# Two decode layers on one core: unread matmuls in three places, and the operand roles of the last up projection

## The chip, the cores and the metric

The kernel runs on one core of one Trainium2 chip. The metric is the device time of one execution in microseconds (us). The core has a matrix engine (PE, TensorE), a vector engine (DVE), a scalar engine (ACT), a general engine (POOL, GpSimd), and a queue (SP) from which nearly all of this kernel's transfers are issued. Matmul results go to PSUM, which the code uses as eight banks of 128 partitions by 512 fp32 numbers; the other engines read them there. A profile of the PE shows two rows, the matmuls (PE) and the loads of the stationary operand (PEld). The granted clock of the PE is shown too: 1.00 is full speed.

## The reference

The model has the sequence attention, feed-forward, attention, feed-forward, with a residual sum around each and one set of weights and caches for both layers. Batch is B = 4, one query token each, D = 512, 32 query heads on 8 key/value heads of 128, 4096 cached positions, feed-forward width F = 1792. All inputs are bf16.

```python
def _A_ref(x, k_cache, v_cache, wq, wo):
    q = heads(x @ wq); k = repeat(k_cache, 4); v = repeat(v_cache, 4)
    p = softmax(einsum("bhqd,bhkd->bhqk", q, k) * Dh ** -0.5)
    return merge(einsum("bhqk,bhkd->bhqd", p, v)) @ wo

def _B_ref(x, w_gate, w_up, w_down):
    return (gelu(x @ w_gate) * (x @ w_up)) @ w_down

x = A_x
x = x + _A_ref(layernorm(x), ...)
x = x + _B_ref(layernorm(x), ...)
x = x + _A_ref(layernorm(x), ...)
x = x + _B_ref(layernorm(x), ...)
```

(`heads`, `repeat` and `merge` stand for the reshapes that are cut here.)

## The kernel before, in words

The key and value caches are 67 MB in all and are read from memory as tiles of 512 KB: 16 positions by 128 numbers on each of 128 partitions. The batch entries go through the layers one after another. The first attention of entry 0 is `attend_first`, its feed-forward is `dense_first`; `attend(b, ...)` works on the second attention of entry b - 1 and the first attention of entry b together, with the keys of an entry kept on the chip between its two attentions; `dense(b, ...)` is the feed-forward of entry b in layer 1. The last entry's second attention is `attend_last`, and the second feed-forward is done once for all four entries in `dense_last`. The order of instructions on every engine is the order of the Python text: the schedule is written by hand (`manual_schedule`), and each engine takes its instructions in that order, waiting on semaphores that the tile framework adds between producers and consumers. The framework keeps tiles apart, so a tile that fills a PSUM bank counts as one thing.

A matmul has a stationary operand (`lhsT`, loaded first) and a moving operand (`rhs`). The kernel uses both ways round for products of activations and weights:

- **weights as the stationary operand** (`mac`, `ffn_in`, `OutProj.heads`, `q_heads`): a 128x128 block of weights is loaded, and a few activation columns, repeated up to 32 or 64 (`wide`), move through it. One matmul for each block; the result has its features on the partitions. For one 512 by 1792 projection that is 14 x 4 = 56 matmuls (`ffn_in`, KF = 14 column blocks by KD = 4 row blocks).
- **weights as the moving operand** (`streamed`, `rows_of` in `dense_last`): a few activation columns are loaded, and 448 columns of weights move. Four such matmuls fill four groups of 32 partitions, j = 0 to 3. For a projection that is 4 x 4 = 16 matmuls. The result has the batch on the partitions and the features along the free axis, and a DVE transpose within 32x32 blocks (line 1365 and 1370) turns it. Because the transpose reads all 128 partitions and only four in each group of 32 are written, the bank is first filled with zeros by ACT (`nothing`, line 346).

`busy(count, unread, ...)` (line 460) issues matmuls of 128 rows by up to 512 columns into a part of PSUM that nobody reads. They have the identity as the stationary operand and the gate weights as the moving one.

**Where the change touches it.**

`dense_first` (line 1260 on) ends with `down`, 56 matmuls of weight blocks into the bank `whole` (tile name y), then one unread matmul of 384 columns into the rest of that same bank. What follows in the main loop is `add_x` (line 396, DVE: XX + y, rounded into xb), then `stats` (line 182: four matmuls of xb against itself for mean and mean square, into a small tile st of the pool ps_sm), then `add_y` (line 401). After that `Early.queries` makes the queries of the second attention, whose first scores set free the key slots for which the SP queue waits (line 489).

`attend_last` (line 1203 on) works through the value tiles with `vals.step`. For all heads but the last, the value tile is the moving operand (line 752, tile so); a DVE transpose (line 760), a reduction (line 767) and a multiplication (line 768) follow and give the head outputs OT2_bf (OT_bf in the profile's names). The last head takes the value tile as the stationary operand (line 819, tile ot) and is scaled in line 651. Output projections: the first three groups of heads go through `RowProj` (line 377, tile yr, weights moving), which `split` takes out of PSUM (ACT line 383, DVE line 384); the last group goes through `OutProj` (line 253, tile y, weights stationary), and `onto` adds the rows to it. Between these stand three calls of `busy` on a bank `spare` of the pool ps_h: four matmuls behind the first two row projections, one behind the third, and one behind the last `proj.heads`.

The last value tiles come from transfers issued late: two heads' tiles as one transfer of 1024 KB each into slots of the query weights (`pump_head`, line 685), and the last head's two tiles into key slots, one whole (line 673) and one in two halves (line 679).

`dense_last` (line 1311 on): the bank u is filled with zeros by ACT, then add_x, stats and add_y for all four entries; DVE prepares the shifts (line 1335) and the variance, POOL takes it to the power -0.5 (line 188). PE runs the 16 gate matmuls (line 1320, tile gr) and the 16 up matmuls (line 1320, tile u), then clears two tiles and turns x back (lines 1355 and 1359, tile xr). DVE: transpose of gr (1365), minus shift (1366), times rstd (1367); ACT: gelu (1369); DVE: transpose of u (1370), minus shift (1371), product with the gelu (1373). PE: the 56 down matmuls (line 1359, tile yo). DVE: the sum with x (1382), and then four small transfers out.

Of the kernel before, what the change touches and what calls it, by code (L numbers as in the profile page):

```python
# [8 lines left out]
FP32 = mybir.dt.float32  # L9
# [6 lines left out]
P = 128  # L16
# [3 lines left out]
QS = P // QD  # L20
WIDE = 32
# [14 lines left out]
def kernel(  # L36
# [13 lines left out]
    nc = tc.nc  # L50
    B, Sq, D = A_x.shape
# [6 lines left out]
    KD = D // P  # L58
    KF = F // P
# [114 lines left out]
        n = shape[0] * shape[1]  # L174
        return (w_sb[:, at].bitcast(FP32)[:, :n].rearrange("p (a b) -> p a b", b=shape[1]))

    def stats(b0, nb):
        st = ps_sm.tile([P, nb, 2], FP32, name="st", tag="sm")
        for i in range(nb):
            b = b0 + i  # L180
            for k in range(KD):
                nc.tensor.matmul(st[:, i], lhsT=xb[:, k, b:b + 1].broadcast_to([P, P]),
                                 rhs=xb[:, k, b:B + 1:B - b],
                                 start=k == 0, stop=k == KD - 1, skip_group_check=True)
        return st
# [159 lines left out]
    def nothing(t):  # L345
        nc.scalar.copy(out=t, in_=qb[:, 0:1].broadcast_to([P, t.shape[1]]))
# [110 lines left out]
    def busy(count, unread, by=None, start=True):  # L457
        rhs = wg_sb[:, 0] if by is None else by
        for _ in range(count):
            nc.tensor.matmul(unread, lhsT=ident_bf[:], rhs=rhs[:, :unread.shape[1]], start=start,  # L460
                             stop=start, skip_group_check=True)

    def down(nb, H_bf, whole):
        y = acc([KD, WIDE], "y2", whole)
        for c in range(KF):
            if c == WD_PARTS[1]:
                busy(2, whole[:, KD * WIDE:], start=False)
            for k in range(KD):
                mac(y[:, k], wd_sb[:, c, k * P:(k + 1) * P], wide(H_bf[:, c, :]),
                    c == 0 and k == 0, c == KF - 1)  # L470
        return y[:, :, :nb]
# [731 lines left out]
    def attend_last(q_bf, norm, before, late):  # L1203
        b = B - 1
        gx, gy = second_groups[b]
        prob2 = {}
        kept2, own2, other2, apart2 = two(b)
        tiles = kept2 + own2 + apart2 + other2
        vals = Values(2, b, tiles, prob2, dst2(b),
                      streamed=[h for h in range(Hkv) if h != tiles[-1][0]],  # L1210
                      paired=[h for h in range(Hkv) if h // 2 != tiles[-1][0] // 2])
        sc2 = [new_scores(early=True)]
        scores(sc2[0], gx, 0)
        ring.pump_tile(late[0], k_tile(gx * GH + 2, 0))
        ring.pump_halves(late[1], k_tile(gx * GH + 3, 0))
        scores(sc2[0], gx, 1)
        q_spread_apart(q_sums(q_bf[:]))
        p0 = soft(sc2[0], norm)
        for _ in range(2):
            before.fill()  # L1220
        before.turn()
        sc2.append(new_scores(early=True))
        scores(sc2[1], gy, 0)
        scores(sc2[1], gy, 1)
        soft_turn(p0)
        before.sum()
        pe0, den0 = soft_swap(p0), soft_den(p0)
        p1 = soft(sc2[1], norm, lasting=True)
        prob2[gx] = (pe0, soft_recip(den0))
        rows = RowProj(o2)  # L1230
        vals.step(8, hold=True)
        soft_turn(p1)
        vals.flush()
        pe1, den1 = soft_swap(p1), soft_den(p1)
        prob2[gy] = (pe1, soft_recip(den1))
        heads = pairs(tiles)
        full = ps_x.tile([P, KF, WIDE], FP32, name="gr", tag="x")
        nothing(full.rearrange("p c r -> p (c r)"))
        nc.scalar.preload_act_table_set("gelu_apprx_tanh_and_others")
        vals.step(4)  # L1240
        rows.heads(heads[0], hp)
        rows.heads(heads[1], hp)
        spare = ps_h.tile([P, 512], FP32, name="spare", tag="h")
        busy(4, spare[:])
        vals.step(2)
        rows.heads(heads[2], hp)
        busy(1, spare[:])
        rows.split()
        vals.step()
        proj = OutProj(o2, B)  # L1250
        proj.heads(heads[3], rep)
        vals.step()
        rows.onto(proj)
        proj.n = Hq - rep
        proj.heads(heads[3] + rep, rep)
        busy(1, spare[:])
        assert vals.left() == 0 and ring.at == len(ring.seq)
        return proj.y, full

    def dense_first(y, scr):  # L1260
        b0, nb, n = 0, 1, 2 * RUN

        def rhs(k):
            return xb[:, k, :n]

        def out_of(i, v):
            nc.vector.tensor_scalar(out=cs_f[:, i], in0=v[:, :, B], scalar1=float(D), scalar2=None,
                                    op0=ALU.mult)
            return v[:, :, b0:b0 + nb]

        add_x(b0, nb, y)
        st = stats(b0, nb)
        add_y(b0, nb, y)
        rstd, mr = ln_scale(nb, st)
        whole = bank("g")
        g = out_of(0, ffn_in(rhs, wg_sb, "g", whole))
        sq = gelu(scr, g, shifts(scr, mr, 0), rstd)
        whole = bank("u")
        busy(6, whole[:])
        u = ffn_in(rhs, wu_sb, "u", whole)  # L1280
        whole = bank("y2")
        busy(4, whole[:])
        u = out_of(1, u)
        H_bf = gate_up(scr, sq, u, shifts(scr, mr, 1), rstd)
        y = down(nb, H_bf, whole)
        busy(1, whole[:, KD * WIDE:], start=False)
        return y

    def dense(b0, y, prev, scr):
        nb = 1  # L1290
# [18 lines left out]
        return turn_rows(y)  # L1309

    def dense_last(y, full):
        up = acc([KF, WIDE], "u")
        nothing(up.rearrange("p c r -> p (c r)"))

        def rows_of(w_sb, full):
            flat = full.rearrange("p c r -> p (c r)")
            for k in range(KD):
# [8 lines left out]
        st = stats(0, B)  # L1326
# [20 lines left out]
        shift(1)  # L1347

        g_rows = rows_of(wg_sb, full)
        u_rows = rows_of(wu_sb, up)  # L1350
        xr = ps_sm.tile([P, P], FP32, name="xr", tag="sm")
        yo = ps_sc.tile([P, P], FP32, name="yo", tag="sc")
        zero = qb[:, 0:1].broadcast_to([P, P])
# [13 lines left out]
        nc.vector.tensor_tensor(out=t[0], in0=t[0], in1=rows(rstd, KF, B), op=ALU.mult)  # L1367
        sq = apart(wq_sb[0], shape, 2)
        nc.scalar.activation(out=sq, in_=t[0], func=ACT.Gelu_apprx_tanh)
        nc.vector.transpose(out=u_rows, in_=u_rows)  # L1370
        nc.vector.tensor_tensor(out=t[1], in0=up[:, :, :B], in1=t[1], op=ALU.subtract)
        H_bf = wq_sb[1][:, 1, :KF * B].rearrange("p (c b) -> p c b", b=B)
        nc.vector.tensor_tensor(out=H_bf, in0=t[1], in1=sq, op=ALU.mult)
# [22 lines left out]
    for b in range(B):  # L1396
        y = dense(b, y, prev, Scratch()) if b else dense_first(y, scr)
        gx, gy = second_groups[b]
        add_x(b, 1, y)
        raw = q_rows(b, gx) if b else None  # L1400
        st = stats(b, 1)
        add_y(b, 1, y)

        if b == 0:
            ring.pump()
            norm = early.queries(b, st)
        else:
            q_bf = q_tile()
            if b == B - 1:
                late = [(2, b) + u for u in two(b)[2]]  # L1410
                room = [[wq_sb[g][:, k].rearrange("p (c d) -> p c d", d=Dh) for k in range(KD)]
                        for g in (gx, gy)]
                pairs_of = [wq_sb[g][:, k:k + NT].rearrange("p t (c d) -> p t c d", d=Dh)
                            for g, k in ((gx, NT), (gy, 0), (gy, NT))]
                ring.pump_head(late[:NT], pairs_of[0])
                prev.fill()
                rest, steps = acc([HG, WIDE], "q"), q_steps(b, gy)
                streamed_part(rest, steps, range(KD // 2))
                banks.back_brief(room[0][0])
            raw = turn_rows(raw)  # L1420
            norm = Norm(st)
            q_round(q_bf, raw, gx, norm)
            if b < B - 1:
                prev.fill()
            norm.root()
            qe = q_sums(q_bf[:])
            if b < B - 1:
                prev.fill()
            else:
                streamed_part(rest, steps, range(KD // 2, KD))  # L1430
                ring.pump_head(late[NT:2 * NT], pairs_of[1])
                ring.pump_head(late[2 * NT:3 * NT], pairs_of[2])
            q_spread(qe)
            if b < B - 1:
                ring.extend(1, b + 1, one(b + 1)[:ahead_of[b + 1]])
                ring.pump()
            else:
                q_bf = q_tile()
                q_round(q_bf, turn_rows(rest), gy, norm)
        if b:  # L1440
            norm.scales()
        if b == B - 1:
            banks.back(room[0][1])

        def qy(b=b, g=gy, norm=norm):
            q_bf = q_tile()
            q_round(q_bf, turn_rows(q_rows(b, g)), g, norm)
            return q_bf[:]

        if b < B - 1:  # L1450
            y, prev = attend(b + 1, qy, prev, norm, early if b == 0 else None)
        else:
            y, full = attend_last(q_bf, norm, prev, late[3 * NT:])
# [32 lines left out]
```

## Time and profile before

| what | value |
|---|---|
| median of 3 runs | 270.87 us (269.98 to 271.11) |
| the profiled execution | 270.28 us, of which the span from first to last instruction is 268.5 us |
| mean granted PE clock over the span | 0.917 |
| PE matmul rows | 199.0 us busy, 4078 matmuls |
| DVE | 176.8 us busy, 435 instructions |
| ACT | 63.2 us busy, 124 instructions |
| memory traffic | 103.10 MB, 384 GB/s on average |
| unread matmuls in `attend_last` (tile spare) | 6, 379 ns median of one row |
| last projections in `dense_last` (line 1320) | gr 16 matmuls, 0.93 us; u 16 matmuls, 0.93 us |
| transpose of u (line 1370) | 0.66 us |

How to read it: a row's duration runs from the start of the first instruction of a group to the modelled end of the last, so neighbouring rows on the PE overlap; the step from one row's start to the next row's start is what a group takes of the PE. The chain of waits is followed back from the last instruction: each of its pieces released the next. DMA issue instructions have a start on the SP queue and a time to landing, counted from that start.

### The profile page before, as it was taken

What the parts mean: (1) busy time and instruction counts of PE and PEld (TensorE: products, weight loads), DVE (VectorE), ACT (ScalarE), POOL (GpSimd) and SP (SyncE); (2) the same over time, 40 slices, a digit from 0 to 9 for tenths busy, and PEclk for the clock granted to TensorE, in tenths of its full rate; (3) what the DMA queues carried; (4) which work ended last, traced back from release to release, by engine and by line L of the source; (5) the groups of instructions that cost most, each with busy time, mean ns of one, the idle gap of its engine ahead of it and who ended that gap; (6) DMA issues with size and microseconds to landing.
All of it is one profiled execution on the core that took longest, in us unless ns stands there. A gap on an engine that the chain in (4) does not pass through costs nothing.

```text
span 268.5 us, 9180 instructions
## 1 busy us (share of the span) xinstructions
PE 199.0 (74%) x4078; PEld 123.6 (46%) x4078; DVE 176.8 (66%) x435; ACT 63.2 (24%) x124; POOL 3.9 (1%) x10
## 2 busy tenths in 40 slices
PE   1395256679689796889688867697799696888893
PEld 1333134568366544447336244364372344544661
DVE  3493952150226899885769997737779987368853
ACT  1001000200404412033315320314235203055620
POOL 2000000000001000000000000000000000000001
PEclk9999557559799979999999988999999989999999
DMA  7999999999996999999999999999999999999920
GB/s 253 420 417 421 417 420 419 411 382 403 407 401 236 391 416 420 417 417 416 377 411 418 417 420 417 417 419 403 403 421 416 417 418 419 416 372 396 416 78 3
DMA packets 32575, 103.10 MB, mean 384 GB/s; under 512 B 2836, under 2 KB 8728, under 8 KB 32536
## 3 DMA queue, kind: packets, MB, share of 16 engines
q1 hardware_dynamic: 32512, 102.51, 95.5%
q8 instruction: 32, 0.52, 0.7%
q14 instruction: 7, 0.06, 0.1%
q10 hardware_dynamic: 24, 0.01, 0.0%
HBM read 102.50 MB, written 0.00 MB: 382 GB/s over the span
## 4 chain that ended last, share of the span: by engine, by line
DMA 48%; DVE 19%; PE 18%; SPq 9%; ACT 2%; issue 2%; DVEq 0%
DMA v_t<-in_A_v_cache_dram 28%; DMA kp<-in_A_k_cache_dram 16%; DVE kp L508 9%; PE sc L563 4%; SPq L149 4%; PE ot L819 4%; DMA wd_sb<-in_B_w_down_dram 4%; SPq L154 3%; PE y L253 3%; PE so L752 2%; PE q L281 1%; DVE q L287 1%; SPq L150 1%; DVE qb L332 1%; DVE pe L573 1%
## 5 line engine op out<-in xcount | busy, mean ns | idle before, releaser
L508 DVE STREAM_TRANSPOSE kp<-kp 128x1024 f32<-128x1024 f32 x64 | 74.1, 1208 | 0.0
L563 PE MATMUL sc<-kp,qb 128*32 128x512 bf16 x512 | 63.4, 429 | 7.3 <-DVE kp L508 3.0
L819 PE MATMUL ot<-pe,v_t 128*128 128x32 bf16 (+1 forms) x1120 | 36.7, 183 | 15.4 <-DMA v_t<-in_A_v_cache_dram 13.1
L819 PEld LDWEIGHTS <-v_t 128*128 128x128 bf16 x1120 | 34.0, 99 | 24.5 <-DMA v_t<-in_A_v_cache_dram 16.1
L563 PEld LDWEIGHTS <-qb 128*32 128x32 bf16 x512 | 21.4, 100 | 39.4 <-issue 21.1
L585 ACT ACTIVATE pe<-sc,nl 128x512 bf16<-128x512 f32 x8 | 5.5, 687 | 85.5 <-DVE pe L582 76.7
L618 PE MATMUL x<-pe,ident_bf 128*32 128x128 bf16 x192 | 5.4, 233 | 12.9 <-DVE pe L593 12.8
L760 DVE STREAM_TRANSPOSE so<-so 128x256 f32<-128x256 f32 (+1 forms) x19 | 11.1, 586 | 5.7 <-PE so L752 5.5
L253 PEld LDWEIGHTS <-wo_sb 128*128 128x128 bf16 x256 | 12.9, 99 | 3.1 <-DMA wo_sb<-in_A_wo_dram 2.5
L253 PE MATMUL y<-OT_bf,wo_sb 128*128 128x64 bf16 x192 | 11.7, 215 | 2.1 <-DMA wo_sb<-in_A_wo_dram 1.8
L618 PEld LDWEIGHTS <-ident_bf 128*32 128x32 bf16 x256 | 5.3, 100 | 16.9 <-issue 14.9
L573 DVE TENSOR_REDUCE pe<-sc 128x1 f32<-128x512 f32 x12 | 8.3, 690 | 6.5 <-PE sc L563 6.4
L752 PE MATMUL so<-v_t,pl 128*32 128x256 bf16 x192 | 9.4, 275 | 3.2 <-DMA v_t<-in_A_v_cache_dram 3.0
L621 ACT CAST pe<-x 128x512 bf16<-128x512 f32 x12 | 7.0, 585 | 19.2 <-PE x L618 19.2
L651 DVE TENSOR_TENSOR OT_bf<-ot,rden 128x8 bf16<-128x8 f32 (+1 forms) x20 | 3.0, 156 | 12.7 <-PE ot L819 12.6
L460 PEld LDWEIGHTS <-ident_bf 128*128 128x128 bf16 x136 | 7.8, 99 | 7.2 <-issue 4.4
L253 PE MATMUL q<-xb,wq_sb 128*128 128x5 bf16 (+1 forms) x192 | 5.5, 170 | 7.5 <-DMA wq_sb<-in_A_wq_dram 7.5
L396 DVE TENSOR_TENSOR xb<-XX,y 128x4 bf16<-128x4 f32 (+1 forms) x9 | 1.6, 173 | 13.6 <-PE y L253 10.8
L752 PE MATMUL so<-v_t,pe 128*32 128x256 bf16 x192 | 7.9, 274 | 2.7 <-ACT pe L621 1.4
L593 DVE STREAM_TRANSPOSE pe<-pe 128x512 bf16<-128x512 bf16 x12 | 8.4, 697 | 2.0 <-ACT pe L585 2.0
L325 PE MATMUL qe<-q_bf,ident_bf 128*32 128x16 bf16 (+1 forms) x272 | 5.5, 175 | 5.6 <-DVE q_bf L307 2.9
L253 PEld LDWEIGHTS <-wq_sb 128*128 128x128 bf16 x192 | 5.2, 98 | 8.1 <-DMA wq_sb<-in_A_wq_dram 8.0
(155 smaller groups left out, 252.0 us busy)
## 6 DMA issues: line engine op xcount, KB each, us to landing
v_t<-in_A_v_cache_dram SPq DMA_DIRECT2D x97, 512.0 KB, 8.5
kp<-in_A_k_cache_dram SPq DMA_DIRECT2D x56, 512.0 KB, 10.1
wq_sb<-in_A_wq_dram SPq DMA_DIRECT2D x2, 2048.0 KB
wo_sb<-in_A_wo_dram SPq DMA_DIRECT2D x4, 1024.0 KB, 11.4
kp<-in_A_k_cache_dram SPq DMA_DIRECT2D x4, 1024.0 KB, 8.6
wq_sb<-in_A_v_cache_dram SPq DMA_DIRECT2D x3, 1024.0 KB, 11.6
wg_sb<-in_B_w_gate_dram SPq DMA_DIRECT2D x1, 1792.0 KB, 12.4
wu_sb<-in_B_w_up_dram SPq DMA_DIRECT2D x1, 1792.0 KB
```

The lines of the kernel that those rows point to most:

```text
L149: dq.dma_start(out=wo_sb[:, i * n:(i + 1) * n], in_=wo_dram[:, i * n:(i + 1) * n])
L154: dq.dma_start(out=wd_sb[:, lo:hi], in_=wd_dram[:, lo:hi])
L253: nc.tensor.matmul(dst, lhsT=lhsT, rhs=rhs, start=first, stop=last, skip_group_check=True)
L460: nc.tensor.matmul(unread, lhsT=ident_bf[:], rhs=rhs[:, :unread.shape[1]], start=start, stop=start, skip_group_check=True)
L508: nc.vector.transpose(out=words, in_=words)
L563: nc.tensor.matmul(sc[s * QS:(s + 1) * QS], lhsT=qb[:, w0:w0 + 2 * W], rhs=kt[:, :, be // 2, :, be % 2], start=(t == 0 and be == 0), stop= ...
L573: nc.vector.tensor_reduce(out=m, in_=sc.rearrange("p c j -> p (c j)"), axis=AX.X, op=ALU.min if norm else ALU.max)
L593: nc.vector.transpose(out=flat, in_=flat)
L618: nc.tensor.matmul(x[a * QS:(a + 1) * QS, s], lhsT=ident_bf[:, s * QS:(s + 1) * QS], rhs=pT[:, a], start=True, stop=True, skip_group_check ...
L752: nc.tensor.matmul(ps[d, :NW * QS], lhsT=x[:, w:w + NW].rearrange("p c h -> p (c h)"), rhs=v[:, i:i + NW, d], start=first and i == 0, stop ...
L760: nc.vector.transpose(out=flat, in_=flat)
L819: nc.tensor.matmul(self.ot[:, s % 2], lhsT=v[:, i, :], rhs=wide(pe[:, s, t * CH + i, :], self.ot.shape[-1]), start=(done == 0 and i == 0), ...
```

## The change

Three edits.

1. `stats` gets an option `spare`, used for entry 0 in the main loop: st is then cut from a whole bank of ps_sm, and one unread matmul of 448 columns goes into the rest of that bank ahead of the four matmuls of the statistics. In `dense_first` the unread matmul of 384 columns behind the down projection goes.
2. In `attend_last` the four unread matmuls behind the second row projection and the one behind the third go. The one behind the last projection stays.
3. In `dense_last` the up projection is done by `ffn_in` with the weights as the stationary operand: 56 matmuls in place of 16. The zeros for its bank (ACT) and the DVE transpose of u go, and the bank is taken after the gate matmuls.

```diff
-    def stats(b0, nb):
-        st = ps_sm.tile([P, nb, 2], FP32, name="st", tag="sm")
+    def stats(b0, nb, spare=False):
+        if spare:
+            whole = ps_sm.tile([P, 512], FP32, name="st", tag="sm")
+            busy(1, whole[:, 2 * QS:])
+            st = whole[:, :2 * nb].rearrange("p (b i) -> p b i", i=2)
+        else:
+            st = ps_sm.tile([P, nb, 2], FP32, name="st", tag="sm")
...
         rows.heads(heads[0], hp)
         rows.heads(heads[1], hp)
-        spare = ps_h.tile([P, 512], FP32, name="spare", tag="h")
-        busy(4, spare[:])
         vals.step(2)
         rows.heads(heads[2], hp)
-        busy(1, spare[:])
         rows.split()
         vals.step()
         proj = OutProj(o2, B)
@@
         proj.heads(heads[3] + rep, rep)
+        spare = ps_h.tile([P, 512], FP32, name="spare", tag="h")
         busy(1, spare[:])
...
         H_bf = gate_up(scr, sq, u, shifts(scr, mr, 1), rstd)
-        y = down(nb, H_bf, whole)
-        busy(1, whole[:, KD * WIDE:], start=False)
-        return y
+        return down(nb, H_bf, whole)
...
     def dense_last(y, full):
-        up = acc([KF, WIDE], "u")
-        nothing(up.rearrange("p c r -> p (c r)"))
...
         g_rows = rows_of(wg_sb, full)
-        u_rows = rows_of(wu_sb, up)
+        up = ffn_in(lambda k: xb[:, k, :B], wu_sb, "u", None)
...
         nc.scalar.activation(out=sq, in_=t[0], func=ACT.Gelu_apprx_tanh)
-        nc.vector.transpose(out=u_rows, in_=u_rows)
         nc.vector.tensor_tensor(out=t[1], in0=up[:, :, :B], in1=t[1], op=ALU.subtract)
...
-        st = stats(b, 1)
+        st = stats(b, 1, spare=b == 0)
```

## The prediction

> **What bounds the kernel now.** I read the page first, then the chain of waits, then the rows in order of time around the three places, then the transfers that land last, and at the end the granted clock. By the page no engine is the bound over the whole span, and the chain is made of all of them:
>
> ```profile
> PE 199.0 (74%) x4078; PEld 123.6 (46%) x4078; DVE 176.8 (66%) x435; ACT 63.2 (24%) x124; POOL 3.9 (1%) x10
> DMA 48%; DVE 19%; PE 18%; SPq 9%; ACT 2%; issue 2%; DVEq 0%
> ```
>
> So each edit is judged in its own stage. The chain of waits (start, us, what) at the three places:
>
> ```profile
> 79.22 0.19 PE y L460
> 79.43 0.18 DVE xb L396
> ...
> 254.62 0.86 PE yr L377 x16
> 255.49 0.97 PE spare L460 x4
> 256.46 0.55 PE so L752 x16
> 257.01 0.43 PE yr L377 x8
> 257.44 0.32 PE spare L460
> 257.76 0.48 PE ot L819 x16
> ...
> 263.11 0.58 DVE u L1370
> 263.71 0.23 DVE wq_sb L1371
> 264.02 0.23 DVE wq_sb L1373
> 264.29 0.98 PE yo L1359 x56
> ```
>
> The reader is to see that the work taken away (the unread matmul at 79.22, the five at 255.49 and 257.44, the transpose at 263.11) is itself a link of the chain each time. What counts is the next-latest release behind each. All times below are those of this profile.
>
> **Part one, the unread matmul at 79 us.** It writes other columns of the bank that holds y, and the DVE's sum at 79.43 waits for it and not for the last down matmul: 0.19 goes. The new one has 448 columns, another bank, and stands on the PE ahead of the statistics. Its cover is the DVE's sum, which would run from 79.24 to 79.41; the statistics start 0.05 behind it, at 79.47. Four rows of 512 columns at 75.60 take 1.02 with their drain, some 0.22 each, so 448 take about 0.19, and the PE is free by 79.3 to 79.4. Without that cover the 0.19 would be back and the part worth nothing. The tile st was last read at 68.7, so its bank keeps nobody waiting. Behind the statistics the chain runs over queries (PE 79.91) and scores (81.81) to the keys for which SP waits: from 82 to 84 us only 39 GB/s arrive, from 86 on 340 to 432 in each two microseconds up to 256. If that stream starts earlier, all behind it moves. Gain 0.19; bounds 0 (a later wait absorbs it) and 0.2. I take 0.19, since the chain leaves this place without a gap.
>
> **Part two, five unread matmuls in the last attention.** From one row's start to the next, the four hold the PE from 255.42 to 256.39, 0.97, and the one from 257.37 to 257.60, 0.23: together 1.20. Next in line is the DVE, which now catches up behind them, and then the last value tiles. The rows of the DVE's pass and of its consumer:
>
> ```profile
> 257.06 0.47 DVE L760 STREAM_TRANSPOSE so<-so 128x256 f32<-128x256 f32 x1 [1.18 <-PE so L752]
> 257.78 0.17 DVE L768 TENSOR_TENSOR OT_bf<-ov,rden 128x4 bf16<-128x4 f32 x1
> 258.08 0.66 PE L253 MATMUL y<-OT_bf,wo_sb 128*128 128x64 bf16 x16
> ```
>
> Step by step, after the edit: the value matmuls so start at 255.42 in place of 256.39 and end at 256.04. The third row projection needs the head outputs written at 255.70 for 0.18, so it starts not at 255.86 but at 256.0, and the first ot at 256.54. The DVE's pass (0.05 from the PE's end to its start at 257.06, then 0.89 to the end of the row at 257.78) runs from 256.09 to 256.98; with 0.06 from DVE to PE, y starts at 257.05, where it started at 258.08 and the PE had 0.07 to spare. The second ot follows 0.50 later at 257.57, against 258.58. Beside it ACT and DVE take the rows out of PSUM: 257.49 to 258.86 now, 256.66 to 258.03 then, needed at 258.05 to 258.09. The last y starts at 258.47 against 259.48. So 1.01 of the 1.20 are left.
>
> The second resource that is late next is memory. Landings of the last three kinds (each issue, KB, us from the issue's start; the issues start at 243.69, 244.86 and, for the second half, 245.72):
>
> ```profile
> wq_sb<-in_A_v_cache_dram SPq DMA_DIRECT2D x1, 1024.0 KB, 11.6
> kp<-in_A_v_cache_dram SPq DMA_DIRECT2D x1, 512.0 KB, 11.7
> kp<-in_A_v_cache_dram SPq DMA_DIRECT2D x1, 256.0 KB, 12.0
> ```
>
> They land at 255.29, 256.56 and 257.72. They would be wanted at 255.42, 256.54 and (eight matmuls of 30 ns into the second ot) 257.81. Now each has about a microsecond in hand; then it is 0.1 or nothing. Part one moves transfers and computing alike. Upper bound of this part 1.20 (the filler's whole time), lower bound 0 (transfers a microsecond later). I take 1.01, as the rows put the transfers just inside.
>
> **Part three, the up projection.** The matmuls of u start at 261.64. In their place come 56 pairs of load and matmul. The same form with the same weights stands in the first feed-forward, at the full clock:
>
> ```profile
> 74.19 1.56 PE L253 MATMUL u<-xb,wu_sb 128*128 128x32 bf16 x56 [0.18 <-DMA wu_sb<-in_B_w_up_dram]
> ```
>
> So u ends at 261.64 + 1.56 = 263.20 instead of 262.57, but unturned. The DVE, free at 263.11, starts the subtraction at 263.24 in place of 263.71; the gelu is done at 263.39; the product starts at 263.55 and the down matmuls at 263.82 against 264.29: gain 0.47. The two clears and eight turning matmuls (262.50 to 263.01) come behind u and end at about 263.66, so they still fit, and ACT's copy of their result is due only at 265.35. The zeros on ACT (0.54 at 258.89) are nobody's wait. The 40 added matmuls lie in the wait for the transpose of gr. The point of no gain is u's end at 263.67, which is (263.67 - 261.64 - 0.15) / 56 = 33.6 ns a pair, where the row gives 25.2 (1.41 to the next row's start). The nearest dearer rows are the 30 ns of 64 moving columns at 258.08. At these the part is worth 0.2; 0.47 is also the upper bound but for 0.1, because the gelu comes next.
>
> **Sum.** 0.19 + 1.01 + 0.47 = 1.67. The profiled execution took 270.28 (span 268.5, 1.8 around it), so 268.6 against its own time. The four times shown are 269.98, 270.28, 270.87 and 271.11; the profiled one lies 0.59 under the median of the runs and 0.28 under the mean of all four, 270.56. I put the sum against that mean: 268.9.
>
> **Rivals.**
>
> *The last value tiles take the filler's place.* For it: a margin of 0.1 or less at three landings, and the slow end of the stream (from 256.5 to 257.5 only 41 to 57 GB/s). Against it: the same profile puts all three inside. Landings half a microsecond later against the computing would leave part two 0.5: total 1.16, time 269.4. Chance 0.22.
>
> *Up without gain,* pairs at 33 ns or a switch between the two forms: total 1.20, 269.4. Against it are the 25.2 ns at 74.19 and at 79.77. Chance 0.08.
>
> *The loads of the weights don't hide (slower).* A load row is 96 ns. If 56 of them stood one behind the other, 5.4 us, u would end at 267.2, and the subtraction would start 3.5 later than now: 1.20 gained less 3.5, time 272.9. It decides for slower from some 80 ns a pair on. Against it: 56 loads take 1.47 together at 74.18. The Trainium skill (TensorE: Matmul & The Clock Gate, Back-to-back issue gap) gives some 81 ns for a pair of load and matmul in a sustained stream at 128 columns; by this estimate u would take 4.5 us and the kernel would lose about 1.4. The row at 74.19 has less than a third of that, for 32 columns, so I give the measured row the weight. Chance 0.03.
>
> *The granted clock falls in the last stage.* The windows view (stretch, us, PE busy, then the other engines, clock, DMA) has:
>
> ```profile
> 91.20:94.60 3.40, 2.08 (x84) 2.03 (x81) 3.26 (x10) 1.18 (x3) 0.00 (x0) 1.00 1.02 412
> 145.80:149.20 3.40, 2.57 (x16) 1.00 (x17) 3.40 (x5) 3.40 (x5) 0.00 (x0) 1.00 1.02 413
> 255.00:258.40 3.40, 3.40 (x68) 1.75 (x57) 1.93 (x7) 0.97 (x2) 0.00 (x0) 1.00 0.42 158
> ```
>
> The clock was 0.50 in the 3.4 us behind the first of these and stayed 1.00 behind the second. The last stage has 3.40 of 3.40 with the filler; without it the new waits of the PE are about 0.2, the rest is work that moves up. A fall of 3.4 us at 0.50 would cost 1.7 and leave no change (270.6); two in a row cost 3.4: slower by 1.7, 272.3. Chance 0.06 in all, a third of it for slower. The Trainium skill (the same page, on the gate's oscillation) asks for a gap in the PE's work of over some 3 us before the clock falls, by which this rival would have no chance and the sum would stay 1.67; the fall at 94.6 came with no gap above 0.94 us, so the trace does not bear that rule out and I keep the chance.
>
> The remaining 0.06 is for what I don't see, half of it slower.
>
> **How the numbers follow.** The forecast has 0.55. About 0.5% (1.35 us) is what a measurement of this kernel can tell from no change: faster lies under 269.5, slower above 272.2. Of the forecast I count 0.50 as faster, 0.05 as same (0.3 less gain, and a median 0.3 higher). Of the first two rivals, at 269.4, half goes each way: 0.15 and 0.15. The clock gives 0.04 same and 0.02 slower, the loads 0.03 slower, the rest 0.03 same and 0.03 slower. Faster 0.65, same 0.27, slower 0.08. The range runs from 268.2 (1.20 + 0.5 + 0.2 gained against the lower half of the times) to 270.3 (a gain of 0.6 against the median's 270.9): 8 in 10.
>
> **What would show it.** Part one: no row of line 460 between the last y and the sum at 79.2, and a row of 448 columns beside that sum. Part two: y of line 253 waits for the multiplication of line 768, not for the PE; if ot or so wait for a transfer, the first rival holds. Part three: one row of 56 matmuls on u of about 1.56, the subtraction right behind it, and yo starting 2.2 behind u's start (now 2.65). A granted clock under 1.00 after 255 us, or a row of u over 2.0 us, would make the prediction wrong.

## The result and the profile after

The changed kernel takes 269.65 us (median of 22 runs, 268.40 to 271.66), the kernel before 270.73 in 22 runs beside it. The ratio is 0.9956 with a 95% interval of 0.9938 to 0.9973, so 1.19 us less (0.73 to 1.68). It is faster, clear of noise, by 0.44%, just inside the 0.5% that the prediction called "same"; 1.67 was forecast. The profiled execution took 270.43, span 268.7, above the median of its kind, where the 270.28 of before lies under its own; the two can't be set against each other as a whole, but their stages can.

The chain of waits of the changed kernel (start, us, what) at the three places. All code lines after 176 have moved: 460 is now 465, 253 is 258, 752 is 757, 819 is 824.

```profile
78.75 0.62 PE y L258 x12
79.40 0.18 DVE xb L401
...
246.01 12.00 DMA kp<-in_A_v_cache_dram
258.06 0.66 PE ot L824 x16
258.71 0.50 PE y L258 x16
...
261.45 0.86 PE gr L1318 x16
262.31 1.51 PE u L258 x56
263.84 0.23 DVE wq_sb L1368
...
264.42 0.98 PE yo L1357 x56
```

All that was to go is gone: there is no unread matmul ahead of the sum at 79.40, no tile spare between the projections, no transpose of u. New is a transfer. The matmuls ot at 258.06 are released by the landing of the last head's first value tile, which was issued 12 us before. The rows in order of time, with the wait in front of a row in brackets:

```profile
254.69 1.06 PE L757 MATMUL so<-wq_sb,pl 128*32 128x256 bf16 x32 [0.36 <-ACT pl L626]
...
256.84 0.62 PE L757 MATMUL so<-wq_sb,pl 128*32 128x256 bf16 x16 [0.23 <-DMA wq_sb<-in_A_v_cache_dram]
...
258.06 0.66 PE L824 MATMUL ot<-pl,kp 128*128 128x64 bf16 x16 [0.17 <-DMA kp<-in_A_v_cache_dram]
...
258.55 0.66 PE L258 MATMUL y<-OT_bf,wo_sb 128*128 128x64 bf16 x16
...
261.38 0.93 PE L1318 MATMUL gr<-wg_sb,xb 128*4 128x448 bf16 x16
```

Both so and ot wait for a transfer. That is the first rival of the prediction. The larger part is lost at so, although the chain names ot: so starts 1.26 behind the start of the row projection (yr, 255.58), where it starts 0.87 behind it when nothing has to land (shown below), and ot 1.22 behind so in place of 1.15.

I read three lengths from row starts, because whole executions differ by more than the change: **S**, from the start of the unread matmul at 79 us (in each kernel the one that stands right behind the last y) to the start of the DVE's sum; **L**, from the 32 value matmuls of the third pair of heads (so, 253.57 before) to the first gate matmul (gr); **F**, from there to the first down matmul (yo). The rows of before that begin and end L:

```profile
253.57 1.06 PE L752 MATMUL so<-wq_sb,pl 128*32 128x256 bf16 x32 [0.36 <-ACT pl L621]
260.88 0.93 PE L1320 MATMUL gr<-wg_sb,xb 128*4 128x448 bf16 x16
```

Before: 0.36, 7.31 and 3.41. After: 0.19, 6.69 and 3.04. The sum of the differences, 0.17 + 0.62 + 0.37 = 1.16, is close to the measured 1.19.

Why is the profiled execution of after not shorter as a whole? Up to 234 us it had lost what it gained later. The windows view of after (stretch, us; busy PE, PEld, DVE, ACT, POOL; clock; DMA share; GB/s):

```profile
224.80:231.40 6.60, 6.22 (x77) 3.24 (x79) 4.96 (x12) 0.58 (x1) 0.00 (x0) 0.50 1.03 418
231.60:268.70 37.10, 29.09 (x778) 19.50 (x771) 23.35 (x81) 14.12 (x29) 1.01 (x1) 1.00 0.70 273
```

The granted clock was 0.50 for these 6.6 us; in the same part of its work before had 1.00 (222.40 to 232.20). The sum of line 396 for entry 3, ahead of the last attention (line 401 after), stands at 241.65 against 240.50, 1.15 late. Of these, 0.26 were there before that stretch (the reduction of line 573, now 578, starts at 221.54 against 221.28); the other 0.89 came in the 20 us that hold it. At the end the kernel is 0.13 late. In all the other profiles below the clock is 1.00 from 224.8 to 231.4, with the edits in and out, though they have stretches at 0.50 elsewhere (changed kernel again: 0.52 on average from 213 to 223); so this stretch belongs to the execution, and I didn't test what sets it. From 231.6 on the clock is 1.00.

### The profile page after: what moved, and what is told of

Its sections match the earlier page's. It is cut to its first block, busy times and chain, and to the rows that moved or that the text cites. A ratio compares the mean times of both kernels' runs of the same rounds, so it can differ in the third digit from the quotient of the medians.

```text
span 268.7 us, 9239 instructions
## 1 busy us (share of the span) xinstructions
PE 199.4 (74%) x4104; PEld 126.2 (47%) x4113; DVE 176.4 (66%) x434; ACT 62.8 (23%) x123; POOL 3.9 (1%) x10
## 2 busy tenths in 40 slices
DMA packets 32575, 103.10 MB, mean 384 GB/s; under 512 B 2836, under 2 KB 8728, under 8 KB 32536
## 4 chain that ended last, share of the span: by engine, by line
DMA 44%; PE 26%; DVE 20%; SPq 5%; ACT 2%; issue 2%; DVEq 0%
DMA v_t<-in_A_v_cache_dram 25%; DVE kp L513 11%; DMA kp<-in_A_k_cache_dram 9%; PE sc L568 7%; PE ot L824 6%; DMA wu_sb<-in_B_w_up_dram 5%; DMA kp<-in_A_v_cache_dram 4%; SPq L149 4%; PE y L258 3%; PE so L757 2%; PE u L258 1%; ACT pe L626 1%; PE q L286 1%; DVE pe L578 1%; DVE q L292 1%
## 5 line engine op out<-in xcount | busy, mean ns | idle before, releaser
L568 PE MATMUL sc<-kp,qb 128*32 128x512 bf16 x512 | 62.5, 432 | 6.6 <-DVE kp L513 2.2
L824 PE MATMUL ot<-pe,v_t 128*128 128x32 bf16 (+1 forms) x1120 | 37.3, 183 | 16.2 <-DMA v_t<-in_A_v_cache_dram 14.1
L258 PE MATMUL y<-OT_bf,wo_sb 128*128 128x64 bf16 x192 | 11.7, 215 | 2.4 <-DMA wo_sb<-in_A_wo_dram 2.2
L757 PE MATMUL so<-v_t,pe 128*32 128x256 bf16 x192 | 8.9, 303 | 2.1 <-ACT pe L626 1.1
## 6 DMA issues: line engine op xcount, KB each, us to landing
wg_sb<-in_B_w_gate_dram SPq DMA_DIRECT2D x1, 1792.0 KB, 12.5
```

What stands on the lines that cost most here:

```text
L258: nc.tensor.matmul(dst, lhsT=lhsT, rhs=rhs, start=first, stop=last, skip_group_check=True)
L568: nc.tensor.matmul(sc[s * QS:(s + 1) * QS], lhsT=qb[:, w0:w0 + 2 * W], rhs=kt[:, :, be // 2, :, be % 2], start=(t == 0 and be == 0), stop= ...
L757: nc.tensor.matmul(ps[d, :NW * QS], lhsT=x[:, w:w + NW].rearrange("p c h -> p (c h)"), rhs=v[:, i:i + NW, d], start=first and i == 0, stop ...
L824: nc.tensor.matmul(self.ot[:, s % 2], lhsT=v[:, i, :], rhs=wide(pe[:, s, t * CH + i, :], self.ot.shape[-1]), start=(done == 0 and i == 0), ...
```

## The experiments

My theory after the result: edits one and three pay nearly as worked out; edit two pays about half, since the landing of the last value tiles comes next, and not the DVE. The rivals were that edit one pays nothing in the end, and that the lost part of edit two lies with the PE or the DVE. The last column is the ratio to the kernel before, run beside it on the same chip (its median was 270.7 for the changed kernel's first row, 271.1 to 271.2 for the others); times in us are worked out with that median.

| kernel | S | L | F | ratio (95% interval) |
|---|---|---|---|---|
| before | 0.36 | 7.31 | 3.41 | 1 |
| changed kernel | 0.19 | 6.69 | 3.04 | 0.9956 (0.9938 to 0.9973) |
| edit one alone | 0.19 | 7.33 | 3.40 | 0.9996 (0.9976 to 1.0015) |
| edit two alone | | 6.50 | 3.41 | 0.9950 (0.9921 to 0.9979) |
| edit three alone | | 7.32 | 3.04 | 0.9982 (0.9958 to 1.0007) |
| ten more unread matmuls at 79 us | 1.98 | 7.32 | 3.41 | 1.0060 (1.0039 to 1.0082) |
| changed, last three transfers left out | | 6.20 | 3.04 | 0.9933 (0.9909 to 0.9957) |
| before, last three transfers left out | | 7.32 | 3.41 | 0.9984 (0.9963 to 1.0005) |
| changed, last transfers cut finer | | 6.26 | 3.04 | 0.9933 (0.9910 to 0.9956) |
| the same again | | 6.48 | 3.04 | 0.9920 (0.9891 to 0.9949) |
| changed kernel, beside it | | 6.75 | 3.04 | 0.9959 (0.9936 to 0.9982) |

### Edit one alone

```diff
-    def stats(b0, nb):
-        st = ps_sm.tile([P, nb, 2], FP32, name="st", tag="sm")
+    def stats(b0, nb, spare=False):
+        if spare:
+            whole = ps_sm.tile([P, 512], FP32, name="st", tag="sm")
+            busy(1, whole[:, 2 * QS:])
...
-        y = down(nb, H_bf, whole)
-        busy(1, whole[:, KD * WIDE:], start=False)
-        return y
+        return down(nb, H_bf, whole)
...
-        st = stats(b, 1)
+        st = stats(b, 1, spare=b == 0)
```

> The kernel before with the first edit alone (unread matmul at 79 us moved behind the down sums into the bank of the statistics). Theory: the DVE's sum no longer waits for it, so from the last row of y to the statistics 0.19 us go, and the whole kernel is 0.2 us shorter, since the keys' stream starts earlier by as much; that is below what the times can tell (0.3 to 0.5), so the profile decides: no row of the unread matmul between y and the sum. Rival: the step goes but a later wait takes it back, time unchanged; the times can't tell the two apart, run delay79 can.

The rows around the unread matmul in this kernel:

```profile
79.31 0.35 PE L465 MATMUL st<-wg_sb,ident_bf 128*128 128x448 bf16 x1
79.50 0.17 DVE L401 TENSOR_TENSOR xb<-XX,y 128x4 bf16<-128x4 f32 x1 [2.40 <-PE y L258]
```

The sum starts 0.19 behind the start of the unread matmul, where before it was 0.36 (79.07 to 79.43), and its wait ends with y of line 258. So this step is 0.17 shorter. The time, 0.1 lower with an interval from 0.65 lower to 0.41 higher, says nothing on whether that arrives at the end.

### Ten more unread matmuls in the same place

```diff
-        busy(1, whole[:, KD * WIDE:], start=False)
+        busy(11, whole[:, KD * WIDE:], start=False)
```

> The kernel before with eleven unread matmuls of 384 columns behind the first down projection where there is one: 10 times 0.16, 1.6 us more on the PE between the last down matmul and the DVE's sum. Theory (what is late at 79 us is late at the end, because the keys' stream starts behind it): time 1.4 to 1.7 higher. Rival (a later wait absorbs it, so the first edit is worth nothing): 0 to 0.8 higher.

The chain of this kernel, and the windows view of a stretch after it (the last column is GB/s):

```profile
79.56 1.81 PE y L460 x11
81.39 0.18 DVE xb L396
```

```profile
84.00:86.00 2.00, 2.00 (x50) 1.38 (x49) 0.65 (x5) 0.00 (x0) 0.00 (x0) 1.00 0.07 16
```

S is 1.62 longer, and the time 1.6 higher (1.06 to 2.22); the transfers, which were back at 338 GB/s in the stretch from 84 to 86 us before, are at 16 there, and at 344 from 86 to 88. L and F are as before. A microsecond more at this place is about a microsecond more at the end, so the 0.17 less of edit one should arrive too; that it does is only inferred from this slope and not shown, as it is too small for the times.

### Edit two alone

```diff
         rows.heads(heads[0], hp)
         rows.heads(heads[1], hp)
-        spare = ps_h.tile([P, 512], FP32, name="spare", tag="h")
-        busy(4, spare[:])
         vals.step(2)
         rows.heads(heads[2], hp)
-        busy(1, spare[:])
```

> The kernel before with the second edit alone (five unread matmuls of the last attention removed). Measure: from the start of the 32 value matmuls of the third pair (so, 253.57 before) to the first gate matmul (gr, 260.88 before), 7.31 us. Theory (the last value tiles' transfers take the filler's place): 6.6 to 6.9, with the PE waiting for a transfer ahead of so or ot; time 0.5 to 0.7 lower. Rival (the DVE's pass is what is late next, as predicted): 6.30, no wait for a transfer; time 1.0 lower.

```profile
255.13 0.61 PE L752 MATMUL so<-wq_sb,pl 128*32 128x256 bf16 x16
256.56 0.65 PE L819 MATMUL ot<-pl,kp 128*128 128x64 bf16 x16 [0.20 <-DMA kp<-in_A_v_cache_dram]
```

L is 6.50, a little better than the theory's 6.6 to 6.9, and there is a wait for a transfer, at ot alone. The time, 1.36 lower (0.57 to 2.14), is above both the 0.81 of L and the theory's 0.5 to 0.7, and its interval holds the rival's 1.0 as well; the profile decides for the transfer here, the times don't.

### The last three transfers left out

Of the last entry's value tiles, the transfer of 1024 KB and the two tiles of the last head are not made. In both versions the matmuls take what lies in the slots.

```diff
         def pump_tile(self, key, v):
-            dq.dma_start(out=v, in_=cache_tile(A_v_cache, *key[1:]))
             self.ready[key] = (v, False)
...
-            for half in (slice(0, CH // 2), slice(CH // 2, CH)):
-                dq.dma_start(out=v[:, half], in_=tile_in[:, half])
             self.ready[key] = (v, False)
...
-                ring.pump_head(late[2 * NT:3 * NT], pairs_of[2])
+                for t, key in enumerate(late[2 * NT:3 * NT]):
+                    ring.pump_tile(key, pairs_of[2][:, t])
```

> The changed kernel without the last three transfers of values (one of 1024 KB, one of 512, two of 256); the matmuls that would read them read what lies in those slots, so the last three heads' sums of the last entry are of other numbers. Theory (these landings are what takes back part of the second edit): no wait of the PE for a transfer after the third pair; from so to gr 6.15 to 6.30 us in place of 6.69 in the changed kernel; against before 1.5 to 1.8 lower in time. Rival (the PE or the DVE's pass is late by itself): 6.5 to 6.7 all the same, time 1.1 to 1.2 lower.

> The kernel before without the same three transfers, as the control for after_nolast; the last three heads' sums of the last entry are of other numbers here too. Theory: the filler covered these landings, so nothing changes: from so to gr 7.31, time within 0.2 of before. Rival (fewer transfers at the end shorten any version): 0.3 or more lower.

Only the last entry's last tiles go through these two functions, so the rest of the traffic stays: 101.00 MB in place of 103.10. The rows of the changed kernel without these transfers:

```profile
256.31 1.04 PE L382 MATMUL yr<-wo_sb,OT_bf 128*4 128x512 bf16 x16
257.18 0.61 PE L753 MATMUL so<-wq_sb,pl 128*32 128x256 bf16 x16
258.33 0.66 PE L820 MATMUL ot<-pl,kp 128*128 128x64 bf16 x16
258.82 0.66 PE L258 MATMUL y<-OT_bf,wo_sb 128*128 128x64 bf16 x16
```

No bracket is left, so follows yr by 0.87, and L is 6.20, as the theory had it. In the control L stays at 7.32. The time, 1.82 lower (1.17 to 2.47), fits it. So edit two is worth 1.12 where nothing has to land, and the filler covered the landings before. The control's time is 0.43 lower, more than the 0.2 expected and in its rival's range, but its interval has zero in it, so whether fewer transfers shorten the rest a little stays open; L and F don't change in it.

### Edit three alone

```diff
-        up = acc([KF, WIDE], "u")
-        nothing(up.rearrange("p c r -> p (c r)"))
...
-        u_rows = rows_of(wu_sb, up)
+        up = ffn_in(lambda k: xb[:, k, :B], wu_sb, "u", None)
...
-        nc.vector.transpose(out=u_rows, in_=u_rows)
```

> The kernel before with the third edit alone (up projection with weights stationary, no transpose, no zeros). Measure: from the first gate matmul (gr) to the first down matmul (yo), 3.41 us before, 3.04 in the changed kernel. Theory: 3.04, that is 0.37 less, of which the 0.10 missing to my 0.47 is the switch from four-row to full weight loads ahead of u; time 0.4 lower. Rival (the part costs or gives nothing): 3.4 and time unchanged.

The chain of this kernel in the last feed-forward:

```profile
260.83 0.86 PE gr L1317 x16
261.69 1.51 PE u L253 x56
263.22 0.23 DVE wq_sb L1367
...
263.80 0.98 PE yo L1356 x56
```

F is 3.04 as in the changed kernel: 0.37 less. In the rows gr starts at 260.76 and u at 261.62, 0.86 apart, where they were 0.76 apart before. The chain now runs through u, and the turned gate result waits for it. The time, 0.49 lower with an interval from 1.14 lower to 0.19 higher, fits and proves nothing more.

### The last transfers cut finer

If landings bind, smaller last pieces should help the changed kernel.

```diff
-        def pump_halves(self, key, v):
+        def pump_parts(self, key, v, parts):
             tile_in = cache_tile(A_v_cache, *key[1:])
-            for half in (slice(0, CH // 2), slice(CH // 2, CH)):
-                dq.dma_start(out=v[:, half], in_=tile_in[:, half])
+            for lo, hi in parts:
+                dq.dma_start(out=v[:, lo:hi], in_=tile_in[:, lo:hi])
...
-        ring.pump_tile(late[0], k_tile(gx * GH + 2, 0))
-        ring.pump_halves(late[1], k_tile(gx * GH + 3, 0))
+        ring.pump_parts(late[0], k_tile(gx * GH + 2, 0), ((0, 8), (8, 16)))
+        ring.pump_parts(late[1], k_tile(gx * GH + 3, 0), ((0, 8), (8, 12), (12, 16)))
...
-                ring.pump_head(late[2 * NT:3 * NT], pairs_of[2])
+                for t, key in enumerate(late[2 * NT:3 * NT]):
+                    ring.pump_tile(key, pairs_of[2][:, t])
```

> The changed kernel with the last transfers cut finer: the 1024 KB one as two of 512, the whole 512 KB one as two halves, the last tile as a half and two quarters. Theory (landings bind): the waits ahead of so and ot get shorter, from so to gr 6.4 to 6.6 in place of 6.69 and 6.50 (the second edit alone); time 1.2 to 1.5 lower than before. Rival (it is the whole stream that ends late, and finer pieces land no earlier): 6.6 to 6.8, time as the changed kernel, 1.1 lower.

> The changed kernel with the last transfers cut finer, once more, beside the changed kernel. Theory: from so to gr 6.2 to 6.35, no wait; time 0.3 to 0.4 under the changed kernel, 1.4 to 1.6 under before. Rival: 6.5 or more as in the changed kernel, times alike.

> The changed kernel as it is, beside the finer cut of the last transfers on the same chip. Theory: from so to gr 6.5 to 6.7 us with waits for the last transfers (6.50 and 6.69 in the two profiles so far), time 1.1 to 1.2 under before. Rival (the landing in the profile of the changed kernel was a single late one): 6.2 to 6.3, no wait.

In the first of the two runs:

```profile
255.72 0.61 PE L757 MATMUL so<-wq_sb,pl 128*32 128x256 bf16 x16
256.87 0.66 PE L824 MATMUL ot<-pl,kp 128*128 128x64 bf16 x16
```

So starts 0.87 behind yr (254.85) and ot 1.15 behind so, with no wait, as in the kernel that leaves the transfers out; L is 6.26, better than the 6.4 to 6.6 expected, and the time 1.82 lower where 1.2 to 1.5 was. In the second run the rows go likewise up to here, and then the last tile is late inside its 16 matmuls, which take 0.92 in place of 0.66 (0.70 in the first run):

```profile
258.02 0.92 PE L824 MATMUL ot<-pl,kp 128*128 128x64 bf16 x16
```

L is 6.48 there, outside the 6.2 to 6.35 expected; the time is 2.17 lower than before, where 1.4 to 1.6 was expected. The changed kernel beside it is late at so (1.16 behind yr) and waits 0.19 at ot again; its second ot takes 0.80 (L 6.75, a little outside the 6.5 to 6.7). The finer cut comes to 269.41 (268.24 to 269.77) and 269.27 (268.33 to 269.92) in six runs each, the changed kernel to 269.65 in 22 and 269.81 in 12. It is faster than before, by 0.67% and 0.80%. Against the changed kernel the two intervals on one chip overlap, so the lead of 0.2 to 0.5 us rests on the stage, where it is 0.2 to 0.5, and on the medians, and not on a verdict. What the cut does can be followed at the last head's first tile: by issue and time to landing its second half comes 2.98 and 3.01 behind the start of the third pair's value matmuls, and ot starts at 2.90. As one piece it would have kept ot waiting for 0.1; as two, the second half is due only eight matmuls, 0.24, later. That it came at 3.0 at all, and not at 3.2 to 3.3 as in the three profiles with edit two and whole tiles, may be the cut or the spread between executions (below); two runs don't tell.

## Why the prediction was right or wrong

**Base and direction.** The mean of the four times, 270.56, was a fair base (270.73 in 22 runs). The direction and the range held, and the measured time is near the 269.4 of the first rival and not the 268.9 of the forecast. The likeliest outcome by its own bound, faster by 0.5% or more, did not come, if barely: it is 0.44%. The range held because it reached down to a gain of 0.6, so it took in the rival as well.

**Part one, 0.19: right.** The profile gives 0.17. The cover held: the statistics start 0.23 behind the sum in both kernels, the 448 columns are no one's wait. That the gain reaches the end is inferred from the slope of 1.6 for 1.6.

**Part two, 1.01: the step that failed** is that "the rows put the transfers just inside". The steps of PE and DVE came out as worked out: without transfers the edit is worth 1.12, and of the 0.11 above my 1.01, 0.10 is the start of so 0.87 behind yr where I had kept 0.97 from the filler's row. The sign that I had named for it, y waiting for the multiplication and not for the PE, shows in no profile: without the transfers the multiplication ends at 258.73 and y starts at 258.82, which is also 0.49 behind ot, the step that it had behind ot before (0.48). The two come so close together that the rows don't say which is later. But the transfers took back a third to a half: of the 1.12 there are 0.62 and 0.56 left in the two profiles of the changed kernel, 0.81 in the edit alone. I had taken the landings of one execution as fixed and their margin of 0.1 as enough. The first tile of the last head (its issue's start plus its time to landing) lies 2.99 behind the start of the third pair's value matmuls in the profile of before (244.86 + 11.7 - 253.57). In six others it was 3.32 (changed kernel), 3.80, 3.17 and 3.21 (edits one, two and three alone), 3.20 (changed kernel again), and 2.64 with the delay at 79 us. The issue stands 8.63 to 8.71 ahead of those matmuls in all seven, so the spread lies in the time to landing, 11.3 to 12.5. The profile that I read was at the early end. Without the transfers ot starts at 2.90; in the three profiles with edit two and whole tiles it starts at 3.17 to 3.37, and L is longer by about as much or a little more, 0.30 to 0.55. So the right term was a spread and not one margin. What makes the landings differ stays open.

**Part three, 0.47: mechanism right, size 0.37.** The 56 matmuls take 1.56, as the row of the first feed-forward gave, and the subtraction follows the end of u directly. What was missing is 0.10 between gr and u. The same 0.10 stands between the row projection and the filler before (0.97 for 16 matmuls) and is not there between the row projection and so (0.86 to 0.87), so I take it for the price of going from narrow stationary loads to full ones; I didn't isolate it, so this is not shown.

**Rivals.** The first held, with 0.22 given to it. Up without gain is excluded by F. Loads that don't hide are excluded by the row of u: 56 pairs in 1.56, 28 ns a pair with the drain of the last. The Trainium skill (TensorE: Matmul & The Clock Gate, Back-to-back issue gap) states 81 ns for 128 moving columns, by which 56 pairs would take an estimated 4.5; with the 32 columns here the trace doesn't agree with such a price. The clock did not fall in the last stage in any of the profiles: in the changed kernel it is 1.00 from 231.6 on, with the PE busy 29.09 of 37.10, and in the others from 232 to the last down matmul.

## What to carry to other kernels

Before a filler is costed as free time on the path, list every arrival that it covers, and give each a spread over executions, not the margin of one profile; a margin under the spread can't be counted on. Where whole executions vary by more than the change, lengths between two rows of one stage show what six or twelve timed runs leave open: F repeated within 0.01 in each kernel here. Where a transfer binds, one profile isn't enough: L came out at 6.50, 6.69 and 6.75 with the same edit two. And where a place is worth too little to time, making it ten times worse measures its slope.

## What I had not expected of the hardware

The landing of the same transfer, counted from the same point of the computing, moved by 1.2 us between executions (2.64 to 3.80) in kernels that are alike up to there but for at most an edit at 79 us. With the last 2 MB cut into pieces of 512, 256 and 128 KB, so and the first ot did not wait in either of two runs, though the bytes and their order are the same; the second ot was still late in one. And between row matmuls with 4 stationary columns and matmuls with 128 behind them stands a steady 0.10 us that no row names, whatever its cause.
